# Attention and max-out FFN on one core: batch 0's loads, turns and value products arranged differently

## The chip, the cores and the metric

The kernel runs on one core of one Trainium2 chip. The metric is the device time of one execution in microseconds, as the median of several runs. TensorE (PE) multiplies matrices and writes to PSUM; VectorE (DVE), ScalarE (ACT) and GpSimd (POOL) work on tiles in SBUF, the first two also on PSUM; SyncE (SP) issues transfers, as ACT and POOL can too. Each engine works through its own instructions in order and waits on semaphores for the others.

## The reference

```python
def _attn_ref(q, k, v, beacon_k, beacon_v):        # B=8, H=8, S=576, D=64; 16 beacons
    k_all = concatenate([beacon_k, k], axis=2)     # 592 keys
    v_all = concatenate([beacon_v, v], axis=2)
    scores = q @ k_all.T / sqrt(D)                 # causal over the 576 keys, beacons always seen
    a = exp(scores - scores.max(-1)); a /= a.sum(-1) + 1e-09
    return a @ v_all

x = attn_out.transpose(0, 2, 1, 3).reshape(4608, 512)
h = maximum(maximum(x @ w1, x @ w2), x @ w3)       # 512 -> 768
out = h @ w_out                                    # 768 -> 512
```

Inputs and output are FP32. The kernel multiplies in BF16 with FP32 sums.

## The kernel before

Heads are handled in pairs (four pairs per batch, 32 in all); two pairs are a "quad", so a batch has quads 0 and 1. For a pair, q and k are loaded with tokens on partitions, cast to BF16, and turned on TensorE (transposes against an identity, L406 and L427) so that the 64 columns of the two heads lie on 128 partitions. Scores are computed key-major: a matmul gives keys on partitions and queries in columns, ScalarE applies the exponential straight from PSUM (L514, L538), and a mask zeroes the upper triangle (L558 on VectorE, L560 on GpSimd). Nothing is subtracted before the exponential. The value product multiplies the exponentials by `ones` (part 0: the sums, 32 rows per head) and by the even and odd columns of v (parts 1 and 2), with four heads side by side in four column groups of TensorE. The sums are inverted on ScalarE as exp(-ln), and VectorE multiplies products by the inverse into `xT`, the FFN's input, already turned. The FFN runs in blocks of 512 tokens: `mm1` for three weights with a running maximum, then `mm2`.

Nothing is scheduled by a planner: `tc.manual_schedule()` keeps the order of the program on every engine. Batches 1 to 7 run in a regular pattern, in which TensorE alternates scores of a pair, value products of a quad (`emit_pv_whole`, L623, in four PSUM banks) and FFN units. Batch 0 is written out by hand in `start` and `first_batch`, since the FFN can't begin before the first attention rows exist.

In batch 0 each pair's rows are loaded as halves of 288 queries or keys. Pairs 0 and 1's first halves come as FP32 (`load_half`, on SP and ACT) and are cast by VectorE and ScalarE. The other three sets, (quad 1, first half), (quad 0, second), (quad 1, second), come by `load_quad` (L265): a transfer issued by POOL that casts to BF16 on its way and leaves one head after the other, so each head is turned by itself, into 64 of the 128 partitions (`turn_part`, L419). `T(p, h, i, bank)` turns half h of q (i = 0) or k (i = 1) of pair p and evacuates it from PSUM (L435); behind a first half of k, a copy places the beacons (L449). `S_(p, g)` computes group g of the scores of pair p, and its exponential. The sixteen groups come in this order: (0,0), (1,0), (2,0), (3,0), (0,1), (1,1), (0,3), (0,2), (1,3), (1,2), (2,1), (3,1), (2,3), (2,2), (3,3), (3,2). They alternate between two pairs of PSUM banks, 0-1 and 2-3 (`sc_psum`). `M(p, g)` masks a group (on POOL, or on VectorE with `True`); `V(t)` casts key tile t of v on POOL (L334).

Value products of batch 0 are made by `emit_pv` (P) for a half of a quad's queries: `P(0, 0)` in banks 6-7, `P(0, 1)` in banks 4-5, both before the last scores, then `P(1, 0)` and `P(1, 1)` behind the last scores in banks 0-1 and 2-3. `invert_sums` (L675, L676) and `multiply` (L686) follow, half by half in the order (0,0), (1,0), (0,1), (1,1). `F()` emits an FFN unit (L739 in the first block). `keep_busy` and `fill` are matmuls without a use.

Of the kernel before, what the change touches and what calls it, by code (L numbers as in the profile page):

```python
# [9 lines left out]
FP32 = mybir.dt.float32  # L10
# [7 lines left out]
def kernel(  # L18
# [13 lines left out]
    nc = tc.nc  # L32
# [27 lines left out]
    n_quad = 2  # L60
# [8 lines left out]

    HEAD_1 = 512  # L70
    groups_0 = [
        [(0, 0, HALF), (1, q_min[1], HALF), (2, q_min[2], HALF)],
        [(0, HALF, S), (1, HALF, HEAD_1)],
        [(1, HEAD_1, S), (4, q_min[4], S)],
        [(2, HALF, S), (3, q_min[3], S)],
# [27 lines left out]
    def head(g, j):  # L103
        return 4 * g + j
# [71 lines left out]
    bT = const.tile([128, PPB, NB_PE], BF16, name="bT")  # L176
    bk32_0 = const.tile([Nb, H, D], FP32, name="bk32_0")
    bk16_0 = const.tile([Nb, H, D], BF16, name="bk16_0")
    bk32_1 = const.tile([NB_PE - Nb, H, D], FP32, name="bk32_1")
    bk16_1 = const.tile([NB_PE - Nb, H, D], BF16, name="bk16_1")  # L180
    bk32 = const.tile([NB_DMA, H, D], FP32, name="bk32")
    bk16 = const.tile([NB_DMA, H, D], BF16, name="bk16")
# [19 lines left out]
    def pv_bank(i, dtype=FP32):  # L202
        return pv_psum[i].tile(dtype)
# [28 lines left out]
    def half_source(g, h, i, j0, n):  # L232
        hs = slice(head(g, j0), head(g, j0) + n)
        src = (q, k)[i][0, hs, HALF * h : HALF * (h + 1)]
        return src.rearrange("h (p r) d -> p h (r d)", r=HR)
# [27 lines left out]
            stage["pair16", p, i] = (rows[:, 0], rows[:, 1])  # L263

    def load_quad(g, h):  # L265
        for i in range(2):
            t16 = quads[g][i][:, 4 * h : 4 * h + 4]
            nc.gpsimd.dma_start(
                out=t16.rearrange("p h r d -> p h (r d)"), in_=half_source(g, h, i, 0, 4)
            )  # L270
            for j in range(PPQ):
                stage["half16", PPQ * g + j, h, i] = (t16[:, 2 * j], t16[:, 2 * j + 1])

    def cast_piece(p, i, cast):
        st = stage["pair", p]
# [65 lines left out]
    def load_w(i, gs=range(n_quad)):  # L341
        wv = (moe_w1, moe_w2, moe_w3)[i].rearrange("(g p e) f -> g p e f", g=n_quad, e=2)
        for g in gs:
            nc.gpsimd.dma_start(out=w_in[i][:, 2 * g : 2 * g + 2], in_=wv[g])
# [6 lines left out]
    def load_beacons(b0, b1, dst, queue=None):  # L351
        for b in range(b0, b1):
            (queue or nc.sync).dma_start(
                out=dst[Nb * (b - b0) : Nb * (b - b0 + 1)],
                in_=beacon_k[b].rearrange("h n d -> n h d"),
            )
# [116 lines left out]

    at = {}

    def at_view(p, t, e, q0, q1):
        spans = []
        off = e * AT_H
        for pieces in groups(p):
            for t_, lo, hi in pieces:  # L480
                if spans and spans[-1][0] == t_ and spans[-1][2] == lo:
                    spans[-1] = (t_, spans[-1][1], hi, spans[-1][3])
                else:
                    spans.append((t_, lo, hi, off))
                off += hi - lo
        for t_, lo, hi, x0 in spans:
            if t_ == t and lo <= q0 and q1 <= hi:
                return at[p][0 : k_rows[t], x0 + q0 - lo : x0 + q1 - lo]
        raise AssertionError

# [79 lines left out]

    def half_passes(cut):
        return [(0, 0, 0, 0, HALF), (1, 1, 0, 0, HALF), (2, 0, HALF, 0, cut), (2, 1, HALF, cut, HALF)]

    passes = [half_passes(q_min[1]), half_passes(192)]
    NPASS = len(passes[0])

    pv_tiles = {}
    unfinished = []  # L580
    ready = [-1]

    def emit_pv(quad, hf, first=0, last=NPASS, apart=False, tiles=None):
        b, g = divmod(quad, n_quad)
        v_sb = v_tiles[b]
        for p in range(PPQ * quad, PPQ * (quad + 1)):
            assert all((p, gi) in masked for gi in range(1 if b == 0 and hf == 0 else NG))
        if first == 0:
            if tiles is not None:
                banks = [tiles[:, i] for i in range(2)]  # L590
            elif apart:
                banks = [ffn_psum.tile() for _ in range(2)]
            else:
                banks = [pv_bank(i) for i in range(2)]
            pv_tiles[quad, hf] = banks
        ps = pv_tiles[quad, hf]
        for part, bank, lo, ca, cb in passes[hf][first:last]:
            qa, qb = hf * HALF + ca, hf * HALF + cb
            ts = [t for t in range(n_kt) if q_min[t] < qb]
            for t in ts:  # L600
                q0 = max(qa, q_min[t])
                n = k_rows[t]
                for j in range(4):
                    lhsT = (
                        ones[0:n]
                        if part == 0
                        else v_sb[0:n, t, head(g, j), part - 1 : D : 2]
                    )
                    nc.tensor.matmul(
                        ps[bank][32 * j : 32 * j + 32, lo + q0 - qa : lo + qb - qa],  # L610
                        lhsT,
                        at_view(PPQ * quad + j // 2, t, j % 2, q0, qb),
                        start=(t == 0),
                        stop=(t == ts[-1]),
                        tile_position=(0, 32 * j),
                    )
        if last == NPASS:
            unfinished.append((quad, hf))


    products = []

    def emit_pv_whole(quad):  # L623
        b, g = divmod(quad, n_quad)
# [42 lines left out]
                ready[0] = 2 * b + 1  # L667

        return finish

    def invert_sums(quad, hf):
        unfinished.remove((quad, hf))
        ps = pv_tiles.pop((quad, hf))
        recip = nrm_pool.tile([128, S], FP32, name="recip")[:, 0:HALF]
        nc.scalar.activation(out=recip, in_=ps[0][:, 0:HALF], func=AF.Ln)  # L675
        nc.scalar.activation(out=recip, in_=recip, func=AF.Exp, scale=-1.0)  # L676
        for n in range(1, NPASS):
            products.append((quad, hf, n, ps, recip))

    def multiply(count=NPASS):  # L680
        for _ in range(min(count, len(products))):
            quad, hf, n, ps, recip = products.pop(0)
            b, g = divmod(quad, n_quad)
            c0 = b % RING * S + hf * HALF
            part, bank, lo, ca, cb = passes[hf][n]
            nc.vector.tensor_mul(  # L686
                xT[:, 2 * g + part - 1, c0 + ca : c0 + cb],
                ps[bank][:, lo : lo + cb - ca],
                recip[:, ca:cb],
            )  # L690
            if g == n_quad - 1 and n == NPASS - 1:
                ready[0] = 2 * b + hf

    hTs = {}
    MID = TOKB // 2
# [172 lines left out]
    def start():  # L868
        keep_busy(8, 480)
        load_half(0, 0, nc.sync)  # L870
        load_half(0, 1, nc.scalar)
        load_half(1, 0, nc.sync)
        load_beacons(0, 1, bk32_0, nc.scalar)
        load_half(1, 1, nc.scalar)
        make_identity(nc, ident)
        nc.gpsimd.memset(tri, 1.0)
        nc.gpsimd.affine_select(
            out=tri,
            in_=tri,
            compare_op=ALU.is_ge,  # L880
            fill=0.0,
            base=0,
            pattern=[[1, 128]],
            channel_multiplier=-1,
        )
        load_quad(1, 0)
        load_quad(0, 1)
        load_quad(1, 1)
        cast_half(0, 0, by_dve)
        cast_half(0, 1, by_act)  # L890
        by_dve(bk16_0, bk32_0)
        turn_part(0, 0, 0, 6, by_act)
        turn_part(0, 0, 1, 7)
        keep_busy(3)
        turn_beacons(0, 1, bk16_0)
        cast_half(1, 0, by_dve)
        cast_half(1, 1, by_dve)
        keep_busy(2)
        turn_part(1, 0, 0, 4)
        turn_part(1, 0, 1, 5)  # L900

    S_, T, M, P, V = emit_scores, turn_part, emit_masks, emit_pv, cast_first_v

    def F(n=1, new_ps=ffn_psum.tile, close=False):
        for _ in range(n):
            assert emit_ffn(END, new_ps, close)

    def first_batch():
# [2 lines left out]
        T(3, 0, 0, 4)  # L911
        load_v(0, 0, nc.vector)
        load_v(0, 1)
        load_beacons(1, B_PE, bk32_1)
        S_(1, 0)
        T(2, 0, 1, 7)
        T(3, 0, 1, 5)
# [27 lines left out]
        M(0, 3, True)  # L945
        M(0, 2, True)
        V(3)
        V(4)
        S_(1, 2)
        fill(6, 2)  # L950
# [1 line left out]
        M(1, 3, True)  # L952
        M(1, 2, True)
        S_(3, 1)
        load_w(1, [0])
        P(0, 0, apart=True)
        S_(2, 3)
        load_w(1, [1])
        M(2, 3)
        S_(2, 2)  # L960
        M(2, 2)
        P(0, 1, 0, 2)
        S_(3, 3)
        M(3, 3, True)
        P(0, 1, 2)
        S_(3, 2)
        M(3, 2, True)
        by_pool(bk16_1, bk32_1)
        load_cast(PPB)
        load_cast(PPB + 1)  # L970
        load_cast(PPB + 2)
        load_w(2)
        load_cast(PPB + 3)
        P(1, 0, tiles=sc_psum.tile())
        P(1, 1, tiles=sc_psum.tile())
        for quad, hf in ((0, 0), (1, 0), (0, 1), (1, 1)):
            invert_sums(quad, hf)
            multiply()
            if (quad, hf) == (0, 1):
                F()  # L980
        F(2)
        turn_beacons(1, B_PE, bk16_1)
        place_beacons(PPB, by_act)
        F(2)
# [125 lines left out]
```

## Time and profile before

| | |
|---|---|
| Median of 3 runs | 285.19 us (284.83 to 285.54) |
| Profiled execution | 286.59 us; its span is 284.9 us |
| Granted TensorE clock | 1.00 over the span |
| Busy: PE, DVE, ACT, POOL | 274.5, 173.7, 159.9, 134.2 us |
| First exponential / first FFN matmul | 7.22 us / 26.27 us |
| HBM read / written | 35.13 / 14.22 MB |

Rows of the timeline give start, length, engine, line, operation, operands and how many were merged; the bracket is the idle time before the first of them and what the profile takes to have ended it. Instructions that overlap in an engine's pipeline are merged into one row, so a row's length is from the first start to the last end. In a view of transfers a queue's row gives packets, MB and the share of sixteen DMA engines' time.

### The profile page before, as it was taken

The page shows a single profiled execution, that of the slowest core. Times are in us where ns is not written, and L with a number is a line of the kernel's source. Part 1 is how long each engine was busy: PE and PEld are TensorE (multiplying, and loading weights), DVE is VectorE, ACT ScalarE, POOL GpSimd, SP SyncE. Part 2 cuts the span into 40 slices and gives each one's busy share as a digit, 9 for nine tenths or more (in the row PEclk, how much of TensorE's full clock was granted, in tenths as well). Part 3 has the DMA queues.
Part 4 walks back from the last instruction along what each step waited for, and adds up shares of the span by engine and source line. Part 5 has one row for each costly group of instructions (what it writes and reads, how often), then busy time and mean ns, then how long its engine had stood idle before and what let it go on. Part 6 is the DMA issues. An engine that isn't in the chain of part 4 may idle for free.

```text
span 284.9 us, 7772 instructions
## 1 busy us (share of the span) xinstructions
PE 274.5 (96%) x3075; PEld 157.3 (55%) x3075; DVE 173.7 (61%) x311; ACT 159.9 (56%) x299; POOL 134.2 (47%) x277
## 2 busy tenths in 40 slices
PE   7976999999999999999999999999999999999994
PEld 3545774555555555555556787555555554444442
DVE  4936785564765748373837383638364847776872
ACT  3975568895668585858585858575766640000000
POOL 7167359558486775457455836583336210000000
PEclk9999999999999999999999999999999999999999
DMA  8999999999998999979999999979845003003004
GB/s 139 204 165 166 170 211 144 239 175 294 286 209 213 226 257 193 183 185 275 252 223 193 257 210 203 205 183 267 206 104 171 0 2 147 4 0 147 2 0 147
DMA packets 85316, 48.84 MB, mean 171 GB/s; under 512 B 64416, under 2 KB 80032, under 8 KB 85280
## 3 DMA queue, kind: packets, MB, share of 16 engines
q1 hardware_dynamic: 78176, 42.22, 65.5%
q0 software_dynamic: 6544, 5.80, 13.9%
q8 instruction: 24, 0.39, 0.6%
q10 hardware_dynamic: 560, 0.33, 0.5%
q14 instruction: 12, 0.10, 0.2%
HBM read 35.13 MB, written 14.22 MB: 173 GB/s over the span
## 4 chain that ended last, share of the span: by engine, by line
PE 81%; DVE 1%; issue 0%; DVEq 0%
PE acc L710 45%; PE acc L762 16%; PE acc L642 11%; PE acc L520 7%; PE acc L406 2%; PE acc L780 0%; DVE hT L728 0%; DVE y L787 0%; DVE qT L442 0%; DVE kT L453 0%; DVEq L453 0%
## 5 line engine op out<-in xcount | busy, mean ns | idle before, releaser
L710 PE MATMUL acc<-xT,w_sb 128*128 128x512 bf16 (+4 forms) x744 | 135.5, 338 | 0.1
L728 DVE TENSOR_TENSOR hT<-hT,acc 128x512 bf16<-128x512 bf16 x102 | 70.0, 688 | 58.2 <-PE acc L710 53.2
L710 PEld LDWEIGHTS <-w_sb 128*128 128x128 bf16 x744 | 69.2, 98 | 59.6
L560 POOL TENSOR_SCALAR_AFFINE_SELECT at_sb<-at_sb 128x256 bf16<-128x256 bf16 (+1 forms) x171 | 61.9, 384 | 81.0 <-ACT at_sb L538 79.8
L538 ACT ACTIVATE at_sb<-acc 128x208 bf16<-128x208 f32 (+3 forms) x140 | 89.5, 737 | 6.7 <-PE acc L520 5.5
L762 PE MATMUL acc<-w_out_sb,hT 128*128 128x512 bf16 (+2 forms) x246 | 48.4, 348 | 0.0
L277 POOL CAST p<-st 96x768 bf16<-96x768 f32 x44 | 34.9, 822 | 0.0
L769 DVE COPY y<-acc 128x512 f32<-128x512 f32 (+1 forms) x35 | 22.0, 629 | 21.2 <-PE acc L762 14.9
L762 PEld LDWEIGHTS <-hT 128*128 128x128 bf16 x246 | 22.6, 98 | 21.7 <-DVE hT L728 1.6
L730 ACT CAST hT<-acc 128x352 bf16<-128x352 f32 x18 | 8.1, 452 | 47.0 <-PE acc L710 47.0
L730 DVE CAST hT<-acc 128x512 bf16<-128x512 f32 (+1 forms) x48 | 26.6, 554 | 9.9 <-PE acc L710 9.6
L520 PE MATMUL acc<-qT,kT 64*128 64x208 bf16 (+1 forms) x336 | 26.6, 280 | 0.4 <-DVE hT L728 0.2
L787 ACT COPY y<-acc 128x320 f32<-128x320 f32 x1 | 0.4, 425 | 46.0 <-PE acc L780 46.0
L642 PE MATMUL acc<-at_sb,v_sb 128*32 128x512 bf16 (+5 forms) x672 | 22.8, 281 | 0.0
L520 PEld LDWEIGHTS <-kT 64*128 64x128 bf16 x336 | 15.4, 94 | 12.7 <-issue 2.5
L665 DVE TENSOR_TENSOR xT<-raw,recip 128x576 bf16<-128x576 f32 x28 | 21.1, 796 | 0.0
L642 PEld LDWEIGHTS <-v_sb 128*32 128x32 bf16 (+1 forms) x672 | 14.6, 97 | 6.7
L322 POOL CAST v_sb<-st 128x1536 bf16<-128x1536 f32 (+2 forms) x21 | 18.3, 894 | 0.0
L652 ACT COPY raw<-acc 128x512 f32<-128x512 f32 x28 | 15.8, 637 | 2.6 <-PE acc L642 2.4
L642 PE MATMUL acc<-at_sb,ones 128*32 128x512 bf16 (+3 forms) x336 | 14.9, 284 | 0.0
L514 ACT ACTIVATE at_sb<-acc 128x1024 bf16<-128x1024 f32 (+2 forms) x16 | 13.1, 864 | 2.6 <-PE acc L505 2.5
L453 DVE COPY kT<-acc 128x576 bf16<-128x576 bf16 x12 | 9.0, 754 | 5.7 <-PE acc L406 4.5
(73 smaller groups left out, 179.4 us busy)
## 6 DMA issues: line engine op xcount, KB each, us to landing
out_dram<-y SPq DMA_DIRECT2D x35, 256.0 KB, 3.5
st<-in_q_dram SPq DMA_DIRECT2D x22, 288.0 KB, 4.4
st<-in_k_dram SPq DMA_DIRECT2D x22, 288.0 KB, 4.7
st<-in_v_dram SPq DMA_DIRECT2D x24, 256.0 KB, 6.0
w_sb<-in_moe_w_dram POOLq DMA_DIRECT2D x6, 384.0 KB, 7.8
q_dram<-p SPq DMA_DIRECT2D x16, 144.0 KB, 2.6
k_dram<-p SPq DMA_DIRECT2D x16, 144.0 KB, 2.5
st<-in_v_dram SPq DMA_DIRECT2D x8, 224.0 KB, 6.2
```

The source lines that it names most:

```text
L277: cast(t16.rearrange("p r h d -> p h r d"), st[0:QP, i * NQ2 : (i + 1) * NQ2].rearrange("p (h r d) -> p h r d", h=2, r=QR),)
L322: cast(v_sb[0:n, t:t1].rearrange("p t h d -> p (t h d)"), st[0:n, (t - t_lo) * H * D : (t1 - t_lo) * H * D],)
L520: nc.tensor.matmul(ps, kTs[p % NT][hs, 128 * t : 128 * t + 128], qTs[p % NT][hs, q0:q1], start=True, stop=True, tile_position=(64 * e, 0),)
L538: nc.scalar.activation(out=both_heads(p, gi)[:, e0:e1], in_=acc[:, first + e0 : first + e1, 0 : g_width(p, gi)], func=AF.Exp, scale=scale,)
L560: nc.gpsimd.affine_select(out=view, in_=view, compare_op=ALU.is_ge, fill=0.0, base=x0, pattern=[[0, 2], [1, hi - lo]], channel_multiplier=-1,)
L642: nc.tensor.matmul(acc[32 * j : 32 * j + 32, bank, lo + q0 - qa : lo + qb - qa], lhsT, at_view(PPQ * quad + j // 2, t, j % 2, q0, qb), sta ...
L665: nc.vector.tensor_mul(xT[:, 2 * g + i, c0 : c0 + S], raw[:, i], recip)
L710: nc.tensor.matmul(ps[:, a:b], w_in[i][:, ct, 128 * ft : 128 * (ft + 1)], xT[:, ct, x0 : x0 + b - a], start=(ct == 0), stop=(ct == n_ct - 1),)
L728: nc.vector.tensor_max(h[:, lo:hi], h[:, lo:hi], ps[:, lo:hi])
L730: (by_act if hi < TOKB else by_dve)(h[:, lo:hi], ps[:, lo:hi])
L762: nc.tensor.matmul(ps[:, lo:hi], hT[:, ft, 128 * tt : 128 * (tt + 1)], w_out_sb[:, ft, lo:hi], start=(ft == 0), stop=(ft == n_ft - 1),)
L769: (by_act if hi < d_model else by_dve)(y[:, lo:hi], ps[:, lo:hi])
```

## The change

- Group 0's three pieces are stored in the order key tile 2, 1, 0 instead of 0, 1, 2, so that tile 0's columns of group 0 and group 1 lie next to each other. Scores and masks of the group follow that order.
- `load_quad` loads FP32 on SP into staging tiles. A new `cast_quad` casts on GpSimd, four instructions for each of the three sets, and lays the two heads of a pair side by side, so that a turn is three transposes of full width instead of six of half width.
- Masks (2,3) and (2,2) go from POOL to VectorE. The beacons of batches 1 to 3 are loaded by POOL with a cast on the way (between `V(3)` and `V(4)`), no longer by SP with a cast by POOL; `load_w(1, [1])` is issued behind the first `load_cast`, `load_w(1, [0])` after scores (2,3).
- Value products are made for a whole quad in four banks: one bank each for sums, even and odd columns of queries 64 to 575, and one for queries 0 to 63 of all three. Quad 0 uses banks 4 to 7, and its pieces by key tile stand between the last scores. Quad 1 uses banks 0 to 3; sums and even columns of key tiles 0, 2 and 3 come first, as these need banks 0-1 and the group (3,3) alone, then the rest. Per quad that is 96 matmuls instead of 116.
- The first 64 queries' sums are inverted by `nc.vector.reciprocal`; the rest by ScalarE, 512 columns for quad 0, and 224 and 288 for quad 1. VectorE multiplies quad 0's 64 and 512 columns, then quad 1's 64, 224 and 288. Three FFN units follow; the first 24 matmuls of the FFN need queries 0 to 255 of both quads.

```diff
     groups_0 = [
-        [(0, 0, HALF), (1, q_min[1], HALF), (2, q_min[2], HALF)],
+        [(2, q_min[2], HALF), (1, q_min[1], HALF), (0, 0, HALF)],
...
     def load_quad(g, h):
+        st = new_stage(("quad", g, h))
         for i in range(2):
-            t16 = quads[g][i][:, 4 * h : 4 * h + 4]
-            nc.gpsimd.dma_start(
-                out=t16.rearrange("p h r d -> p h (r d)"), in_=half_source(g, h, i, 0, 4)
+            nc.sync.dma_start(
+                out=st[0:QP, i * NQ2 : (i + 1) * NQ2].rearrange("p (h x) -> p h x", h=4),
+                in_=half_source(g, h, i, 0, 4),
             )
+
+    def cast_quad(g, h):
+        st = stage.pop(("quad", g, h))
+        for i in range(2):
             for j in range(PPQ):
-                stage["half16", PPQ * g + j, h, i] = (t16[:, 2 * j], t16[:, 2 * j + 1])
+                a = 4 * h + 2 * j
+                t16 = quads[g][i][:, a : a + 2].rearrange("p a r d -> p (a r d)")
+                x0 = i * NQ2 + j * NQ2 // 2
+                by_pool(
+                    t16.rearrange("p (r e d) -> p e r d", r=HR, e=2),
+                    st[0:QP, x0 : x0 + NQ2 // 2].rearrange("p (e r d) -> p e r d", e=2, r=HR),
+                )
+                stage["half16", PPQ * g + j, h, i] = (
+                    t16.rearrange("p (r x) -> p r x", r=HR),
+                )
...
+    def pv_heads(quad):
+        bank = pv_tiles[quad][3]
+        for part in range(3):
+            out = bank[:, part * HEAD : (part + 1) * HEAD]
+            pv_matmuls(quad, part, out, 0, 0, HEAD, True, True)
+
+    def pv_rest(quad, part, ts, last):
+        bank = pv_tiles[quad][part]
+        for t, lo, hi, _ in sorted(spans_of(PPQ * quad), key=lambda x: x[1]):
+            if t in ts:
+                q0 = max(lo, HEAD)
+                pv_matmuls(
+                    quad, part, bank[:, q0 - HEAD : hi - HEAD], t, q0, hi, t == 0, t == last and hi == S
+                )
...
+    def invert_heads(quad):
+        recips[quad] = nrm_pool.tile([128, S], FP32, name="recip")
+        nc.vector.reciprocal(recips[quad][:, 0:HEAD], pv_tiles[quad][3][:, 0:HEAD])
+
+    def invert_rest(quad, q0, q1):
+        recip = recips[quad][:, q0:q1]
+        sums = pv_tiles[quad][0][:, q0 - HEAD : q1 - HEAD]
+        nc.scalar.activation(out=recip, in_=sums, func=AF.Ln)
+        nc.scalar.activation(out=recip, in_=recip, func=AF.Exp, scale=-1.0)
...
-        load_quad(1, 0)
-        load_quad(0, 1)
-        load_quad(1, 1)
+        for g, h in ((1, 0), (0, 1), (1, 1)):
+            load_quad(g, h)
+        for g, h in ((1, 0), (0, 1), (1, 1)):
+            cast_quad(g, h)
...
-        load_beacons(1, B_PE, bk32_1)
...
         V(3)
+        load_beacons(1, B_PE, bk16_1, nc.gpsimd)
         V(4)
...
         S_(3, 1)
-        load_w(1, [0])
-        P(0, 0, apart=True)
-        S_(2, 3)
-        load_w(1, [1])
-        M(2, 3)
-        S_(2, 2)
-        M(2, 2)
-        P(0, 1, 0, 2)
-        S_(3, 3)
-        M(3, 3, True)
-        P(0, 1, 2)
-        S_(3, 2)
-        M(3, 2, True)
-        by_pool(bk16_1, bk32_1)
-        load_cast(PPB)
...
-        P(1, 0, tiles=sc_psum.tile())
-        P(1, 1, tiles=sc_psum.tile())
-        for quad, hf in ((0, 0), (1, 0), (0, 1), (1, 1)):
-            invert_sums(quad, hf)
-            multiply()
-            if (quad, hf) == (0, 1):
-                F()
-        F(2)
+        open_pv(0, [acc[:, i] for i in (4, 5, 6, 7)])
+        pv_heads(0)
+        pv_rest(0, 0, (0, 1, 2, 3, 4), 4)
+        S_(2, 3)
+        load_w(1, [0])
+        M(2, 3, True)
+        pv_rest(0, 1, (0, 1, 2), 4)
+        S_(2, 2)
+        M(2, 2, True)
+        pv_rest(0, 2, (0, 1, 2), 4)
+        S_(3, 3)
+        M(3, 3, True)
+        for part in (1, 2):
+            pv_rest(0, part, (3,), 4)
+        S_(3, 2)
+        M(3, 2, True)
+        load_cast(PPB)
+        load_w(1, [1])
...
+        for part in (1, 2):
+            pv_rest(0, part, (4,), 4)
+        invert_heads(0)
+        invert_rest(0, HEAD, S)
+        multiply_heads(0)
+        for part in (1, 2):
+            multiply_rest(0, part, HEAD, S)
+        tiles = [sc_psum.tile() for _ in range(2)]
+        open_pv(1, [tiles[i // 2][:, i % 2] for i in range(4)])
+        for part in (0, 1):
+            pv_rest(1, part, (0, 2, 3), 4)
+        pv_rest(1, 0, (1, 4), 4)
+        pv_heads(1)
+        invert_heads(1)
+        multiply_heads(1)
+        invert_rest(1, HEAD, HALF)
+        pv_rest(1, 1, (1, 4), 4)
+        pv_rest(1, 2, (0, 1, 2, 3, 4), 4)
+        for part in (1, 2):
+            multiply_rest(1, part, HEAD, HALF)
+        ready[0] = 0
+        invert_rest(1, HALF, S)
+        for part in (1, 2):
+            multiply_rest(1, part, HALF, S)
+        ready[0] = 1
+        F(3)
         turn_beacons(1, B_PE, bk16_1)
```

## The prediction

> **What bounds the kernel now.** I read the page first, then the chain of waits, then the timeline of TensorE, ScalarE, VectorE and GpSimd over the first 35 us, the windows there, the DMA view, and the program's order with what each wait is for. The page:
>
> ```profile
> span 284.9 us, 7772 instructions
> q8 instruction: 24, 0.39, 0.6%
> PE 81%; DVE 1%; issue 0%; DVEq 0%
> ```
>
> TensorE is the bound: the chain is nearly all PE, and after 26.27 us its timeline has no idle stretch above 0.2 us. So the change, which ends there, is worth the shift of that moment, the first FFN matmul (L739). TensorE just before it:
>
> ```profile
> 22.44 0.63 PE L609 MATMUL acc<-at_sb,ones 128*32 128x288 bf16 x14
> 25.03 0.27 PE L609 MATMUL acc<-at_sb,ones 128*32 128x208 bf16 x4 [1.96 <-DVE xT L686]
> 25.16 1.18 PE L609 MATMUL acc<-at_sb,v_sb 128*32 128x288 bf16 x54
> 26.27 0.94 PE L739 MATMUL acc<-xT,w_sb 128*128 128x256 bf16 x7
> ```
>
> 1.96 us idle inside quad 1's value products. The releaser named is a product (L686), but by the program's order that matmul (PE's 706th instruction) waits only for the second instruction of mask (3,3) (L558), which ended at 22.36. The wait is not on data. The DMA view of 22.7 to 23.8 has
>
> ```profile
> q8 instruction: 1, 0.02, 5.4%
> ```
>
> The page's 24 packets, 0.39 MB for TensorE's 6152 instructions, make 64 bytes each and 256 to a packet. One such packet started at 22.78, landed at 23.73, and work resumed at 25.03. I read the idle as a late instruction fetch: one line of 256 is used up in 3.4 us of value products.
>
> Ahead of that ScalarE's sixteen exponentials (L514) set the pace:
>
> ```profile
> 7.22 1.94 ACT L514 ACTIVATE at_sb<-acc 128x1024 bf16<-128x1024 f32 x2 [0.81 <-PE acc L505]
> 9.31 5.39 ACT L514 ACTIVATE at_sb<-acc 128x1024 bf16<-128x1024 f32 x6 [0.15 <-PE acc L505]
> 20.72 1.30 ACT L514 ACTIVATE at_sb<-acc 128x992 bf16<-128x992 f32 x2 [1.24 <-PE acc L505]
> ```
>
> They run almost without idle from 7.22 to 19.48; then 1.24 us are lost, since scores (3,3) stand on TensorE behind products that wait for the last cast of v (L334, ends 20.1). The last exponential ends at E = 22.0.
>
> **The change, part by part.**
>
> *Loads.* Six POOL issues (0.67 to 0.81 us each, 1.84 to 5.97) become six on SP at about 0.45 (its two h loads took 0.89). The FP32 bytes read are the same 1.77 MB. At 280 GB/s (window 3 to 4, FP32 loads) they need 6.3 us from 4.0, one per 1.05: last at 10.3. At 200 GB/s it would be 12.8, and the last turn, at 12.59, would be 1.1 late; at the higher rate everything is in time. I take 0, because that window moved the same kind of row (768 bytes); bounds 0 and +0.7 (0.4 of slack before exponential (0,3)). The v loads stand behind them on SP, but their gate, a VectorE memset at 8.24, holds them anyway.
>
> *Casts.* Twelve of 96x384 on GpSimd: half of 96x768 (823 ns, L277) is 0.41, the 128x512 row (610 ns and up) bounds from above; 0.45, in all 5.4 us from about 6.0. GpSimd was idle 7.2 us there, so they fit before the first v cast at 13.17.
>
> *What they lie beside.* This is the dear part. VectorE masks beside GpSimd casts:
>
> ```profile
> 9.35 0.41 DVE L558 TENSOR_TENSOR at_sb<-at_sb,tri 128x256 bf16<-128x256 bf16 x2
> 16.09 0.79 POOL L334 CAST v_sb<-st 128x512 bf16<-128x512 f32 x1
> 16.13 0.84 DVE L558 TENSOR_TENSOR at_sb<-at_sb,tri 128x256 bf16<-128x256 bf16 x2
> ```
>
> Alone, two masks take 0.41. Beside a cast two take 0.84, the second ending with the cast; this happens at 13.26, 15.04 and 16.33, each 0.62 to 0.66 for one that needs 0.2. Evacuations from PSUM (L453) took 745 to 758 ns with GpSimd busy or not. The casts now cover VectorE's stretch from 6 to 11.5, where it is nearly always busy and carries, ahead of the evacuation that scores (0,1) need, one SBUF cast (L247), three beacon copies (L449), a memset and masks (0,0). The three masks come back to back and wait half a cast to a whole one, 0.22 to 0.45 each; the other five, spread among evacuations, wait 0 to 0.15 each: 0.7 to 2.1. The evacuation (ends 10.34) has 0.25 of that in hand before scores (0,1) at 10.93, the rest of the 0.59 being turns on TensorE. So exponential (0,1), at X = 11.36 before, comes at 11.8 to 13.2; I take the middle, 12.5, since the rows show waits of both sizes.
> The Trainium skill, "SBUF — State Buffer", section "Who interferes with whom", lets only the port pair that VectorE and GpSimd share contend, as an exclusive lock; "VectorE: DVE Perf Modes", "Why PSUM operands drop a tier", says that an operation with a PSUM operand cannot use both ports. The masks and L453 agree; by that rule PSUM evacuations stay free, and X stays under 13.2.
>
> *Exponentials.* From X twelve remain: four of 0.92 start to start, four of 0.89, four of 0.40: E = X + 8.85. Full-width turns halve 72 transposes (0.45 per 12), hidden beside the exponentials: 0. Without collisions E is set by TensorE's order instead: S(2,3) at 17.4, products, S(3,3) at 19.2 once exponential (2,3) is read, then 1.3: E = 20.9. With X = 12.5, E = 21.35, and I add 0.35 since mask (1,2) is now late on VectorE and S(2,3) stands behind products that wait for it: 21.7. Before: 22.0.
>
> *Masks (2,3), (2,2)* to VectorE: 0.7 us in its 4.77 idle; 0. *Beacons* to POOL: three issues of 0.55 to 0.68 between the fourth v cast (17.45) and the fifth's data (19.48); 0, or 1:1 what exceeds 2.0. *load_w(1, [1])* behind the first load_cast: needed with the seventh FFN unit, 34.7; 0. The removed bk cast (0.60, after 1.68 of waiting) lets load_cast issue near 20.6 instead of 24.3, ahead of its use.
>
> *Products and normalizing.* A whole quad's products take 2.25 (the chain's L642 pieces), from E-0.35: done by E+2.1. Longer is the chain after E: Ln and Exp of 512 (L658 0.62 to 0.70, L660 0.68 for 576): E+1.2. Two products of 512 (1.1 ns per column by 112 and 288 columns of L686, 0.62 start to start): E+2.45. Quad 1's reciprocal and head product: 0.5; the reciprocal of 64 columns is nowhere in the trace, between 0.2 (a 96-column product is 0.25) and 0.5 (as 288 columns); 0.25 taken, as it is nearer the first. Two of 224 columns at 0.31: E+3.6, handovers 0.15. Three FFN matmuls (0.117 each) go ahead of that, so the FFN starts in effect at E+3.4. Before it was E+4.27, and without the 1.96 it could not have been before 24.5, the last product it needs. A TensorE idle of 1.3 us stays, ended by VectorE.
>
> *Fetch.* 36 transposes and 40 value matmuls fewer, each with its weight load: the FFN begins at the 676th instruction, not the 828th, and the line that ended at 706 now ends in its 16th matmul, near 26.8. The late line came 6.3 us after TensorE had reached the 450th instruction (18.77), one line earlier; that instruction is now a product behind scores (3,3), near 20.5, which gives 26.8. I take 0; bounds 0 and +1.96.
> The Trainium skill, "Runtime: NRT & Kernel Launch", section "Instruction fetch mechanics", has blocks of 256 instructions too, but calls the cost of crossing one mostly hidden; by that rule the idle is no fetch, and rival E follows.
>
> **Sum.** FFN at 21.7 + 3.4 = 25.1 against 26.27: -1.17. Profiled: span 284.9 to 283.7, and with the 1.7 around it 286.59 to 285.4. That run is 1.40 above the median of the three, 285.19; from the median: **284.0**. X from 11.8 to 13.2 gives FFN 24.65 to 25.8: 283.6 to 284.7.
>
> **The rivals.**
> - *No collisions* (B): GpSimd and VectorE run side by side. Against it, the three masks. E = 20.9, FFN 24.3, -1.97: 283.2. Chance 0.18.
> - *The evacuations wait as well* (C, slower): six of them stand before scores (0,1), and a whole cast of 0.45 for each puts X from 12.5 to 15.2, E to 24.05, FFN to 27.45: 286.4. Against it L453; for it, no evacuation in batch 0 ran beside a cast, and a starved VectorE also feeds TensorE's order. Even is X = 14.0, slower by 0.86 is X = 14.9. Chance 0.20.
> - *The gain exists only in the profile* (D): the idle may be longer under the profiler. All 1.40 of the difference to the median could be it; the timed kernel then starts the FFN at 24.87, after at 25.1: 285.4, and without collisions 284.6; both no change. Chance 0.12.
> - *The idle comes again* (E): its cause is not the fetch but something in quad 1's products that the profile doesn't name, and it returns there. Products then end at E+4.1, FFN 25.8, -0.5: 284.7, no change. Against it, the packet at 22.78. Chance 0.08.
> - *My forecast* (A): 0.42, some 0.30 of it below 284.3.
>
> This measurement can tell about 0.3% (0.86 us). Faster: 0.30 + 0.18 = 0.48. Same: 0.12 + 0.12 + 0.08 = 0.32. Slower: 0.20. Signs are mixed, so the range is wide: 283.0 holds B, 286.4 half of C.
>
> **What would show it.** Right: masks (0,0) at 0.4 to 0.7 beside quad casts, PSUM evacuations still 0.45; exponential (0,1) near 12.5; no idle of 2 us within L602; FFN near 25.1, its wait ended by a product on VectorE. Wrong: an idle inside the FFN's first 16 matmuls with a q8 packet beside it; a turn that waits for a quad cast; exponential (0,1) past 14.0; or a load_cast pair landing after its turn near 30, which would give back what was won.

## The result

The changed kernel takes 287.81 us (median of 6 runs, 286.40 to 289.43); the kernel before, run beside it on the same chip, 284.87 us (6 runs, 284.73 to 285.54). The ratio is 1.0102, 95% interval 1.0059 to 1.0146. It is slower by 2.9 us, outside the range, and not the 1.2 us faster that was forecast. Ratios here and below leave out executions that took over 1.5% longer than the fastest of the same kernel. The six times follow the mean granted TensorE clock of their executions: 286.40 at 0.999, 286.69 and 287.31 at 0.994, 288.30 at 0.988, 289.38 and 289.43 at 0.982.

The profiled execution took 286.69 us. Its page, with the lines that answer to those of before, and the row of the granted clock:

```profile
span 285.0 us, 7624 instructions
PEclk9799999999999999999999999999999999999999
q8 instruction: 23, 0.38, 0.6%
PE 81%; DVE 1%; issue 0%; DVEq 0%
```

TensorE is still the chain. But in the second slice, 7 to 14 us, its clock was at 0.7: the trace has half clock from 10.05 to 13.46 us and full clock on both sides. In TensorE's windows (length, busy time, clock, DMA share, GB/s):

```profile
7.00:8.00 1.00, 0.59 (x10) 1.00 1.13 237
9.00:10.00 1.00, 0.68 (x8) 1.00 1.13 227
10.00:11.00 1.00, 0.90 (x8) 0.52 1.14 234
```

What TensorE lacked from 7 to 10 us was data. The first of its idle pieces waits for VectorE's cast of a `load_half` transfer, which itself waited 0.57 us for the landing, the later ones for quad casts:

```profile
7.45 0.30 PE L440 MATMUL acc<-ident,h 96*128 96x96 bf16 x3 [0.41 <-DVE h L246]
9.25 0.30 PE L440 MATMUL acc<-ident,quad 96*128 96x96 bf16 x3 [0.17 <-POOL quad L279]
```

The quad casts on GpSimd wait for landings, 1.25 us apart; the last cast ends at 14.65. The first four of the twelve:

```profile
7.44 0.95 POOL L279 CAST quad<-st 96x384 bf16<-96x384 f32 x2 [5.55 <-DMA st<-in_q_dram]
8.69 0.96 POOL L279 CAST quad<-st 96x384 bf16<-96x384 f32 x2 [0.29 <-DMA st<-in_k_dram]
```

The exponentials, which ran almost without idle from 7.22 us before, now stall one after another; the last row ends at E = 23.20, against 22.02 before:

```profile
8.12 2.03 ACT L531 ACTIVATE at_sb<-acc 128x1024 bf16<-128x1024 f32 x2 [1.40 <-PE acc L522]
10.75 1.02 ACT L531 ACTIVATE at_sb<-acc 128x1024 bf16<-128x1024 f32 x1 [0.60 <-PE acc L522]
12.31 1.02 ACT L531 ACTIVATE at_sb<-acc 128x1024 bf16<-128x1024 f32 x1 [0.54 <-PE acc L522]
13.76 1.02 ACT L531 ACTIVATE at_sb<-acc 128x1024 bf16<-128x1024 f32 x1 [0.42 <-PE acc L522]
21.90 1.30 ACT L531 ACTIVATE at_sb<-acc 128x992 bf16<-128x992 f32 x2 [0.23 <-PE acc L522]
```

The fourth row is exponential (0,1), the X of the prediction: 13.76. Behind E there is no idle of 2 us within the value products any more, and the FFN's first units wait for products on VectorE:

```profile
25.73 0.38 PE L749 MATMUL acc<-xT,w_sb 128*128 128x256 bf16 x2 [0.33 <-DVE xT L650]
26.81 2.38 PE L749 MATMUL acc<-xT,w_sb 128*128 128x256 bf16 x18 [0.71 <-DVE xT L650]
```

Two matmuls of 0.117 go first, so the FFN starts in effect at 26.81 - 0.23 = 26.58.

### The profile page after: what moved, and what is told of

Read it like the earlier page. It is cut to its first block, busy times and chain, and to the rows that moved or that the text cites. A ratio compares the mean times of both kernels' runs of the same rounds, so it can differ in the third digit from the quotient of the medians.

```text
span 285.0 us, 7624 instructions
## 1 busy us (share of the span) xinstructions
PE 276.4 (97%) x2999; PEld 156.7 (55%) x2999; DVE 175.5 (62%) x312; ACT 159.3 (56%) x297; POOL 136.3 (48%) x282
## 4 chain that ended last, share of the span: by engine, by line
PE 81%; DVE 1%; issue 0%; DVEq 0%
PE acc L720 45%; PE acc L772 16%; PE acc L675 11%; PE acc L537 7%; PE acc L419 2%; PE acc L790 0%; DVE hT L738 0%; DVE y L797 0%; DVE qT L455 0%; DVE kT L466 0%; DVEq L466 0%
## 5 line engine op out<-in xcount | busy, mean ns | idle before, releaser
L577 POOL TENSOR_SCALAR_AFFINE_SELECT at_sb<-at_sb 128x256 bf16<-128x256 bf16 x168 | 61.2, 386 | 80.3 <-ACT at_sb L555 79.1
L772 PEld LDWEIGHTS <-hT 128*128 128x128 bf16 x246 | 22.6, 98 | 21.7 <-DVE hT L738 1.6
L749 PE MATMUL acc<-xT,w_sb 128*128 128x256 bf16 x96 | 11.7, 273 | 1.1 <-DVE xT L650 1.0
```

The source lines that it names most:

```text
L577: nc.gpsimd.affine_select(out=view, in_=view, compare_op=ALU.is_ge, fill=0.0, base=x0, pattern=[[0, 2], [1, hi - lo]], channel_multiplier=-1,)
L772: nc.tensor.matmul(ps[:, lo:hi], hT[:, ft, 128 * tt : 128 * (tt + 1)], w_out_sb[:, ft, lo:hi], start=(ft == 0), stop=(ft == n_ft - 1),)
```

## The experiments

Theory: the time is lost at the start of batch 0, where the FP32 quads land late and TensorE, short of work, also loses its clock; products and normalizing bring nothing. Rivals: the casts beside VectorE cost it, or the products do, or the issuing queue does. Each kernel was compared with the kernel before on the same chip (medians there 284.86 to 285.06).

**The kernel before, again** (no edit).

> The kernel before, unchanged, profiled again. The timed executions of before have a median of 284.87 us, which with the 1.69 us that lie around the profiled span leaves a span of 283.2, while the profiled one had 284.9 and 1.96 us of TensorE idle inside L609. Theory 'the idle was an accident of that execution': here the span is 283.0 to 283.6, no idle of over 1 us stands in L609, and the FFN starts near 24.5. Rival 'it belongs to every execution': an idle of about 2 us stands there again, the FFN starts near 26.3 and the span is 284.9.

284.80 us over 10 runs, ratio 0.9999 (0.9984 to 1.0015). TensorE in this second profiled execution:

```profile
23.63 0.27 PE L609 MATMUL acc<-at_sb,ones 128*32 128x208 bf16 x4 [0.55 <-DVE xT L686]
24.87 2.86 PE L739 MATMUL acc<-xT,w_sb 128*128 128x256 bf16 x24
```

The idle that the forecast wanted to remove was 1.96 us in one execution and is 0.55 in the next. With E = 22.02 in both, the FFN follows at E+2.85 here and at E+4.25 there.

**The products part alone.**

```diff
 the kernel after, but:
-            nc.sync.dma_start(out=st[...], in_=half_source(g, h, i, 0, 4))   # FP32, SP
+            nc.gpsimd.dma_start(out=t16..., in_=half_source(g, h, i, 0, 4))  # casting, as before
-            cast_quad(g, h)
```

> The changed kernel with the old loads: quads come by POOL's casting transfers, one head after the other, and are turned with half width; group order, value products, normalizing and the rest as changed. Theory 'the loads are the cost': exponential (0,1) is back at 11.4 (13.8 in the changed kernel), TensorE is at full clock throughout, the last exponential ends near 21.0, the FFN starts near 24.4, and the time is 284.4 to 285.2, against 284.9 before and 287.8 changed. Rival 'the products are the cost': 286.4 or more.

284.9 us over 10 runs, ratio 1.0000 (0.9976 to 1.0025): no cost and no gain. The time is as expected; E and the FFN come later than expected:

```profile
24.30 0.38 PE L735 MATMUL acc<-xT,w_sb 128*128 128x256 bf16 x2 [0.32 <-DVE xT L636]
25.39 2.82 PE L735 MATMUL acc<-xT,w_sb 128*128 128x256 bf16 x22 [0.71 <-DVE xT L636]
```

Its last exponential ends at 21.78 and the FFN starts in effect at 25.16, E+3.38. Value products are done earlier than before, and TensorE then waits 1.03 us for VectorE: an idle for an idle.

**The loads part alone.**

```diff
 the kernel before, with load_quad and cast_quad of the kernel after (FP32 on SP, GpSimd casts, full-width turns)
```

> The kernel before with the new loads alone: quads as FP32 on SP, cast by GpSimd, turned with full width. Theory 'the loads are the cost': first quad cast at 7.4, exponential (0,1) at 13.5 to 14, last cast of v near 22 and behind it scores (3,3), so the last exponential ends near 24; 287 to 289, with intervals of halved TensorE clock and some us of scatter. Rival 'the products are the cost': 284.9 to 285.3 with no scatter.

289.66 us over 4 runs (288.13 to 291.78), ratio 1.0176 (1.0121 to 1.0230). The whole loss is here, more than expected and more than the full change has. X is 13.81 and the clock was half from 10.64 to 14.06; in its quad 1 products the idle is back, 1.20 us.

**More work for TensorE, the loads as they are.**

```diff
-        turn_part(1, 0, 1, 5)
+        turn_part(1, 0, 1, 5, None, 2)
-        T(2, 0, 0, 6)
+        T(2, 0, 0, 6, None, 1)
-        T(2, 0, 1, 7)
+        T(2, 0, 1, 7, None, 1)
-        T(3, 0, 1, 5)
+        T(3, 0, 1, 5, None, 1)
```

Five matmuls of no use are added to the kernel after, ahead of turns that wait.

> The changed kernel with five more matmuls without a use ahead of four turns, in TensorE's idle stretches between 6.6 and 10 us. Theory 'idle TensorE loses its clock': the granted clock is 1.00 in all executions, the scatter of 3 us goes (to under 0.5), and the median falls from 287.8 to 286.0 to 286.5; what is left above 284.9 is the late loads. Rival 'the scatter comes from the transfers': clock and scatter as in the changed kernel, 287 to 288.5.

286.79 us over 4 runs (286.70 to 287.27), ratio 1.0073 (1.0058 to 1.0088), clock 0.999 or 1.000 in each. By the medians five matmuls more make the kernel 1.0 us faster, a little less than expected, and its scatter falls from 3 us to 0.6. Its windows just before and in the stretch in which the kernel after was at half clock:

```profile
9.00:10.00 1.00, 1.00 (x11) 1.00 1.14 224
10.00:11.00 1.00, 0.90 (x12) 1.00 1.12 228
11.00:12.00 1.00, 0.94 (x12) 1.00 1.15 218
12.00:13.00 1.00, 0.85 (x12) 1.00 1.23 198
```

So by the medians the clock was worth about 1 us of the 2.9, and 1.9 remain with the clock full. The two intervals overlap, so the size is rough: the changed kernel's executions at 0.994 and 0.999 (286.40 to 287.31) were no slower than these, and what the full clock took away are those at 0.988 and 0.982 (288.30 to 289.43). The quads are still late (the casts start at 7.49 and end at 15.45). In the profiled execution X falls to 13.09, but a later turn waits for the last quad, and E is 23.78, later than the changed kernel's 23.20.

**The same loads on GpSimd's queue.**

```diff
 the kernel after, in load_quad:
-            nc.sync.dma_start(
+            nc.gpsimd.dma_start(
```

> The kernel after the change, with the six quad loads still FP32 and still cast by GpSimd, but issued on GpSimd's queue as before the change instead of SP's. Theory (the SP queue delivers the quads late): the landings come 0.85 us apart again, 7.0 to 11.4, the first quad cast starts near 7.1, exponential (0,1) at 12.0 to 12.6 instead of 13.8, the TensorE clock is full from 7 us on, and the time is 285.0 to 285.7. Rival 1 (it is the FP32 write into SBUF that is slow, whatever the queue): landings 1.25 us apart, exponential (0,1) near 13.7, time 286.5 to 288. Rival 2 (the casts beside VectorE cost the time, not the landings): landings as before the change, but exponential (0,1) at 13 or later, masks (0,0) at 0.6 us and more each, time 286 or more.

288.39 us over 4 runs, ratio 1.0104 (1.0064 to 1.0144). The queue is acquitted, and the theory as written was wrong on that point: landings are 1.27 us apart,

```profile
7.33 0.95 POOL L279 CAST quad<-st 96x384 bf16<-96x384 f32 x2 [1.29 <-DMA st<-in_q_dram]
8.60 0.95 POOL L279 CAST quad<-st 96x384 bf16<-96x384 f32 x2 [0.32 <-DMA st<-in_k_dram]
```

and X is 14.04. Rival 1 holds, with a time 0.4 us above its upper end. The casting transfers of the kernel before, on the same queue, read the same bytes in 0.87 us each (landings from 7.02 to 11.39) and write half as many.

**The same bytes over more partitions.**

```diff
 the kernel after, in load_quad:
-                out=st[0:QP, i * NQ2 : (i + 1) * NQ2].rearrange("p (h x) -> p h x", h=4),
-                in_=half_source(g, h, i, 0, 4),
+                out=st[:, i * 576 : (i + 1) * 576].rearrange("p (c x) -> p c x", c=3),
+                in_=two_heads.rearrange("(c p r) d -> p c (r d)", c=3, r=HR),
```

> The kernel after the change, but each quad load writes 128 partitions of the FP32 stage instead of 96: the same queue, the same six transfers of 288 KB, the same runs of 768 bytes and the same casts of 96x384. (The casts then pick up rows of other places, so batch 0's q and k are other rows of the input; no work is left out.) Theory (the pace of 1.25 us is set on the writing side by the partitions that are written): landings 0.85 to 0.95 us apart, last near 11.5, exponential (0,1) at 12.3 to 12.9, time 285.3 to 286.3 and the half-clock stretch gone or shorter. Rival (an FP32 load of 768-byte runs is this slow wherever it writes): landings 1.25 apart as before, exponential (0,1) near 13.7, time 286.5 to 289.

285.63 us over 10 runs (284.98 to 287.86), ratio 1.0030 (1.0001 to 1.0058). The landings are 0.89 to 0.91 us apart (1.04 the last). The casts run back to back, and the windows move 40% more per us:

```profile
7.19 5.62 POOL L280 CAST quad<-st 96x384 bf16<-96x384 f32 x12 [5.30 <-DMA st<-in_q_dram]
```

```profile
7.00:8.00 1.00, 1.00 (x16) 1.00 1.11 336
8.00:9.00 1.00, 0.96 (x14) 1.00 1.11 326
```

X is 12.40 and E = 20.54 + 1.30 = 21.84, as good as with the products part alone (21.78). So the pace was set where the data is written, by 96 partitions against 128: 294,912 bytes in 0.90 us are 328 GB/s, in 1.25 us 236. The edit also changes which rows are read (two whole heads, not halves of four), which no run separates; but the casting transfers read the old rows in 0.87 us each. The Trainium skill, "SBUF — State Buffer", section "Door 1: The DMA port swizzle", says that partitions 0 to 63 lie behind 8 of the 16 write ports and 64 to 127 behind the other 8. By that rule two thirds of a 96-partition transfer go through half the ports, and the rate is three quarters: 246 GB/s as an estimate from 328. The trace's 236 agrees within about 4%. Half clock is gone from the profiled execution, but three of the ten runs were at 287.6 to 287.9 with the clock at 0.988; seven at full clock have a median of 285.34.

The rate of 280 GB/s that the prediction used came from a window of the kernel before that was not steady. In halves (length, clock, DMA share, GB/s):

```profile
3.00:3.50 0.50, 1.00 1.08 346
3.50:4.00 0.50, 1.00 1.03 214
```

Its q and k loads, of 144 KB, wrote 96 partitions too. So partitions alone do not tell them from the quads, and why they moved more than 236 GB/s for half a us stays open.

**Less work for TensorE, the loads of before.**

```diff
 the kernel before:
-        T(0, 1, 0, 6, None, 1)
+        T(0, 1, 0, 6)
 and so for T(0, 1, 1, 7), T(2, 1, 0, 6) and T(2, 1, 1, 7)
```

> The kernel before, without the four matmuls of no use that stand ahead of turns (0,1) and (2,1) of each half; nothing else is left out and the loads are untouched. Theory (the clock follows how busy TensorE is in the 3 us before): TensorE's busy share between 7 and 10 us falls below the 0.79 of before, a stretch of 3.4 us at half clock follows between 9 and 14 us, the exponentials behind it come up to 1.2 us later, and the times scatter: 285.3 to 287.5. Rival (the half clock came from the new loads or the casts, not from idle time): clock 1.0 throughout, time 284.9 or a few tenths less, since four matmuls are gone.

285.05 us over 10 runs (284.58 to 286.84), ratio 1.0020 (1.0001 to 1.0039). In its profiled execution the clock was half from 13.95 to 17.36, though nothing of the loads was touched: idle TensorE loses it by itself. Three of the ten runs lie at 286.6 to 286.84 with the clock at 0.992 to 0.994. The stretch came later than expected. ScalarE waits for TensorE twice around it, where it waited 0.17 and 0.18 us before:

```profile
15.57 1.30 ACT L514 ACTIVATE at_sb<-acc 128x992 bf16<-128x992 f32 x2 [0.63 <-PE acc L505]
17.27 3.13 ACT L514 ACTIVATE at_sb<-acc 128x1024 bf16<-128x1024 f32 x4 [0.40 <-PE acc L505]
```

E is 22.27, 0.25 later than in both profiles of before. The FFN starts at 24.31 all the same, earlier than in either, since here no idle stands inside quad 1's products.

**Quad 1's head products first**, with the products part alone.

```diff
         M(3, 3, True)
+        invert_heads(0); multiply_heads(0)
...
         open_pv(1, ...)
+        pv_heads(1); invert_heads(1); multiply_heads(1)
+        multiply_rest(0, 1, HEAD, S); multiply_rest(0, 2, HEAD, S)
```

> The products part alone (loads and turns as before the change), with both 64-column reciprocals and head products moved on VectorE ahead of quad 0's products of 512, into time in which it waits. Theory (after the last exponential VectorE's row of reciprocals and products is what the FFN waits for; 0.84 us of it moves out): products of 512 at 22.95 as before, those of 224 at 24.2 instead of 24.95, the second group of FFN matmuls at 24.7 instead of 25.4, time 284.1 to 284.4. Rival (something later in the kernel, a load or a turn of batch 1, sets the end whatever the start of the FFN): time 284.9 with TensorE idle elsewhere by what was saved.

285.02 us over 11 runs, ratio 1.0007 (0.9998 to 1.0016). No gain, and for neither reason given: the products row was shortened, and another idle stood up, ended by nothing that the profile shows:

```profile
24.47 0.65 PE L588 MATMUL acc<-at_sb,v_sb 128*32 128x176 bf16 x22 [0.94 <-issue]
```

Counted in the program's order, it stands behind TensorE's first 351 matmuls. So do the idle of 1.96 and 0.55 in the kernel before and the 1.20 in the loads part alone, whatever work comes there. The products part alone and the kernel with less work for TensorE pass the same place without idle.

**The stream moved by 20 matmuls.**

```diff
 the kernel before:
-        keep_busy(8, 480)
+        keep_busy(28, 137)
```

> The kernel before, with the eight opening matmuls of no use (480 columns each) cut into 28 of 137 columns: the same columns in all, 20 matmuls more in front of everything. Theory (the idle in quad 1's products stands at a place in TensorE's instruction stream, the 351st matmul, and not at a piece of work): the idle of 0.5 to 2 us, if the profiled execution has it, is again ahead of the 351st matmul, which is now 20 matmuls earlier in the work, near 22.4 us instead of 23.1. Rival (it belongs to the work, to a wait that the trace does not name): ahead of the 371st matmul, near 23.1. Time 284.9 in both, within 0.3.

The idle stands again behind 351 matmuls ("ahead of the 351st" in the expectation), 20 earlier in the work:

```profile
25.84 0.26 PE L609 MATMUL acc<-at_sb,v_sb 128*32 128x176 bf16 x4 [3.42 <-issue]
```

3.42 us this time, in the longest of the ten executions, and half clock follows from 26.10 to 29.52. The place belongs to the instruction stream. The kernel as a whole was slower: 286.37 us over 10 runs, ratio 1.0036 (1.0012 to 1.0060), which neither side expected.

The packets of queue q8, which the prediction took for instruction fetches, say what ends the idle. In the window 23.4 to 24.5 of this trace, inside the idle:

```profile
q8 instruction: 1, 0.02, 5.5%
```

Its packet lands at 24.43. In the five profiles with the idle, this packet lands at 22.30 (before, second profile), 23.03 (head products first), 23.73 (before), 24.43 (here) and 25.39 (loads part), and TensorE resumes 1.30 to 1.44 us behind each. In the two that pass the place without idle it had landed at 20.86 and 21.69, 2.46 and 1.48 us before TensorE got there. So by all seven the idle is a wait for this packet. Why it comes when it does, at 21.33 in one execution of the kernel before and at 22.78 in the other, stays open.

**Both**: the head products first, and 79 matmuls more in front.

```diff
 the kernel with the head products first:
-        keep_busy(8, 480)
+        keep_busy(87, 44)
```

> The kernel with the products part alone and quad 1's head products first, with the eight opening matmuls of no use cut into 87 of 44 columns, so that the 351st matmul is now where TensorE waits for the last exponentials anyway. Theory (what the earlier start of the FFN gains there is eaten by the idle at the 351st matmul): the idle falls together with that wait, the products run through, the FFN starts at 24.2 to 24.5 and the time is 284.2 to 284.6. Rival (the gain is given back later, whatever the start of the FFN): FFN at 24.2 to 24.5 and time 284.9 to 285.1. Either way the 79 extra matmuls run before the first q and k have landed and cost nothing.

285.02 us over 12 runs, ratio 0.9988 (0.9972 to 1.0003). No long idle is left, and the FFN runs through from 24.44:

```profile
24.44 2.79 PE L735 MATMUL acc<-xT,w_sb 128*128 128x256 bf16 x21 [0.76 <-DVE xT L636]
...
178.75 0.88 PE L523 MATMUL acc<-qT,kT 64*128 64x208 bf16 x12 [0.24 <-DMA kT<-k_dram]
```

The rival holds: the FFN starts as both sides expected, and the time does not follow. Against the second profile of before, the same FFN copies come 0.37 us earlier up to 170 us. Then the scores at 170.53 take 1.27 us where those of before take 0.92, the next ones wait for the DMA that brings kT back from DRAM, as the second line shows, and the head start is gone by 179. No version here beats the kernel before.

## Why the prediction was wrong

- **Loads.** This step failed. It took 0, bounds 0 to 0.7, from a rate of 280 GB/s in one early window: casts from near 6.0, one landing per 1.05, last at 10.3. Measured: first landing 7.4, one per 1.25, last at 13.6. With the landings at 0.90 apart, X is 12.40; the kernel after has 13.76. The term was 1.36, of which about half (13.76 to 13.09) went when the clock was kept up, though E did not gain by that. A window of 1 us, 346 GB/s in one half and 214 in the other, was read as a steady rate. The step's own dearer case, 200 GB/s with the last landing at 12.8, was nearer and got no weight, and the prediction's sign of being wrong, a turn that waits for a quad cast, is what the trace shows. The step also missed that the FP32 quads delay a transfer that was there before: VectorE's last `load_half` cast, which waited for nothing before, waits 0.57 us for its landing. The first exponential comes at 7.95 to 8.35 in the five kernels with FP32 quads, at 7.22 to 7.78 in the other profiles. That SP's last three issues each waited for an earlier landing (to 4.08, 5.16 and 7.40) was missed too, and cost nothing: the 128-partition loads have the same waits.
- **The clock.** It was in no step and in no rival. The late turns leave TensorE idle by 0.10 to 0.41 us at a time, and half clock for 3.41 us follows; five of the six executions have a mean clock below 0.999.
- **Casts.** Right: 5.62 us for twelve, 0.47 each, against 0.45.
- **Collisions.** Masks (0,0) took 0.90 us for three, and 1.19 where the casts ran without a break, against 0.59 alone; evacuations from PSUM stayed at 0.45. That is 0.10 and 0.20 each, below the 0.22 to 0.45 of the step, and rival C (evacuations wait) is refuted. With the loads 0.90 apart X = 12.40 is near the 12.5, but partly by luck: the first exponential was late itself (7.96), and from it to X 4.44 us passed, against 4.14 and 4.25 in the two profiles of before. And it moved E by only 0.06 us (21.84 against 21.78): E is not X + 8.85 when X is early, since TensorE's order sets it. Rival B was right on that, though its E of 20.9 was not reached.
- **Exponentials.** From 13.76 they gave E = 23.20, X + 9.44, where the step had X + 9.20.
- **Products and normalizing.** FFN at E+3.4 was right: E+3.38 in the changed kernel, in the products part alone and with 128 partitions. The reciprocal was mis-sized, 0.55 and not 0.25, just outside its bound of 0.5, so that both products of 224 columns end at E+3.86 and not E+3.6. The FFN start came out by luck in part: its third matmul waits for the first of the two alone (26.81). Counted from the fourth, which starts at 27.11 behind the second, it would be E+3.56.
- **The baseline.** This step failed as well: E+4.27 for before (4.25 with E = 22.02) was one execution's accident, and E+2.85 the second's. Measured against that, E+3.4 is a loss of 0.53, not a gain of 0.87. Rival D gave just this number (FFN of before at 24.87), with a chance of 0.12, though not for its reason: the second execution was profiled too. The sum of this way closes: E later by 1.18 and the FFN by 0.53 make 1.71; VectorE's copies for the FFN come, from 40 us on, 1.70 later than in the second profile of before, and stay so to the last. That the change is worth the shift of the FFN's start, the prediction's first step, was right here.
- **Fetch.** Right: 351 matmuls now end with the FFN's 14th (the 16th was forecast), and no idle stands there. That the idle belongs to the stream and ends with a q8 packet is shown; that the packet holds instructions remains an argument from its size of 256 of them. The Trainium skill, "Runtime: NRT & Kernel Launch", section "Instruction fetch mechanics", calls the cost of a crossing mostly hidden. The traces agree for the rest of the kernel: before has no idle above 0.20 us after the FFN's start, while 22 more packets land. At this one place the cost was 0.55 to 3.42 us in five of twelve profiles.
- **Beacons, masks, load_w.** Nothing in the trace waits for them, as forecast.

The forecast of 25.1 for the FFN missed 26.58 by 1.48: 1.26 in X, 0.24 from X to E, and nothing behind. That the timed median is 1.1 us over the profiled execution goes with the clock: that one had one half-clock stretch, others up to three by their mean clock.

## What to carry to other kernels

Read a transfer's rate from loads of the same size that write the same number of partitions, over several of them and not over 1 us, and compare bytes written, not bytes read: a casting load that writes half may be the faster one although it looks dearer. Before an idle stretch of one profile is entered as a gain, take a second profile of the same kernel. Where work is taken from the engine that sets the end, ask whether its idle pieces come so close together that it loses its clock. Judge a version by its timed runs: the kernel with five more matmuls was faster than the changed one by its median, and slower in its one profiled execution.

## What the runs showed of the hardware

- Half clock came in stretches of 3.413 us or twice that, after intervals in which TensorE was 72 to 77% busy by the trace (four kernels), in the changed one without an idle piece above 0.41 us. In a fifth, the shifted stream, it followed the idle of 3.42 us. The Trainium skill, "TensorE: Matmul & The Clock Gate", section "Why this matters for your kernels", asks that no gap exceed some 3 us; the fifth profile agrees, but in the other four short gaps were enough. Which share decides is open: one interval of before was 43% busy, at 22.6 us, and kept its clock.
- A 96-partition FP32 load moved 236 GB/s from either queue, a 128-partition one of the same bytes 328.
- The idle behind 351 matmuls differs from execution to execution of one kernel, 0.55 and 1.96 us. What ends it is shown as "issue" or as a product long done; in all five profiles it ends 1.30 to 1.44 us behind the landing of a q8 packet.
